# Fused attention, MLP and top-1 experts: output rows turned in 32 by 32 blocks and written in 128-byte pieces, in place of TensorE transposes

## The chip, the cores and the metric

One core of one Trainium2 chip runs the whole program in one launch. The metric is device time in microseconds (us) of that core, the median of several runs. Engines are named TensorE (PE in the rows, its weight loads PEld), VectorE (DVE), ScalarE (ACT), GpSimd (POOL) and SyncE (SP, which here only issues transfers).

## What is computed

```python
# q, k, v: (2, 12, 448, 64); x: 896 tokens x 768
scores = cap * tanh(q k^T / 8 / cap);  attn = softmax(scores);  x = attn v      # rows of 768
x = relu(x @ w_in) ** 2 @ w_out                                                # w_in 768x2048, w_out 2048x768
xn = x / (norm(x, axis=-1) + 1e-6);  en = expert_emb / (norm + 1e-6)             # 8 experts
logits = xn @ en.T / tau;  e = argmax(logits);  gate = softmax(logits)[e]
out[t] = gate[t] * (relu(x[t] @ w1[e]) @ w2[e])                                # w1 768x1024, w2 1024x768
```

All is float32. Each product is made of three reduced-precision products (high by high, high by low, low by high part), so every weight is split into a high part `wh` and a low part `wl` first.

## The kernel before

The 896 tokens are two batches of 448 (b = 0, 1). Activations lie with features on the 128 partitions and the 448 tokens along the free axis. The stages follow each other on TensorE: attention of batch 0 (paced by VectorE, to about 70 us); attention of batch 1 woven into the MLP of batch 0 (to 235 us); the MLP of batch 1 (to 366 us); the expert of batch 0 (`expert(0)`, to 434 us); the expert of batch 1 (`expert(1)`, to the end). For each batch the kernel takes the expert that most tokens chose, runs all 448 tokens through it, and later overwrites the tokens that chose another: they are gathered from `x2d` in DRAM by an indirect transfer, run through their own expert as an extra tile (products `xo`, `xy`, woven in as "x" chunks), and scattered into `out` by GpSimd (`extra_scatter`).

- **MLP.** `h` = 16 products of 6 x 3 matmuls, `y` = 6 products (d = 0..5) of 16 x 3 matmuls. After each y product ScalarE copies PSUM to `xf` (128 features x 448 tokens). Four feature products later in the next d, `rows(d, xf)` makes `x2h`, `x2l` for the experts, and also the token-major rows: four TensorE transposes `x2t`, a ScalarE copy `xr`, one transfer to `x2d` from ScalarE's queue, and four ScalarE squares that sum each token's squares (`ssp`).
- **Router** (`router(b)`, a generator that `interleave` advances between matmuls): 12 matmuls `lg`, a copy `lgs`, four small transposes `lt`, then a chain of small VectorE and ScalarE steps to the gate and the choice of the expert.
- **Expert.** `e` = 8 products of 6 x 3 matmuls, `z` = 6 products of 8 x 3. After each z product ScalarE copies it to `of`; in the next d, `rows(d, of)` makes four TensorE transposes `ot`, one VectorE multiplication by the gate into `orow`, and for two values of d one transfer to `out` from ScalarE's queue. The last two d of batch 1 go through `merged_rows`, which merges the extra tile with TensorE's help instead of the scatter.
- **Weights.** SyncE loads chunk n+7 into `wf` once VectorE has made the low part of the chunk that had this buffer (4 or 8 chunks earlier); ScalarE (or VectorE in the second MLP) casts it to `wh`, VectorE subtracts to `wl`, three chunks ahead of TensorE. Each `yield` between matmuls emits one such step (`drip`). In the MLP of batch 0 the weights come wide (`wr`) and their float32 form is stored once to DRAM (`wk`).

The order of instructions on an engine is the order in which the code emits them; each engine goes through its own list in order, so a queue that waits at one instruction holds what stands behind it. SyncE and ScalarE issue transfers to two hardware queues.

Of the kernel before, what the change touches and what calls it, by code (L numbers as in the profile page):

```python
# [8 lines left out]
F32 = mybir.dt.float32  # L9
# [11 lines left out]
def kernel(  # L21
# [59 lines left out]

    x2d = [dram.tile([NT, DM], F32, name="x2d", tag="x2d")]


# [486 lines left out]
    def mlp(b):  # L571
# [30 lines left out]
        def rows(d, xf):  # L602
            nc.vector.tensor_copy(x2h[:, d], xf)
            nc.vector.tensor_tensor(x2l[:, d], xf, f32(x2h[:, d]), op=ALU.subtract)
            tp = ps.tile([P, NC, P], F32, tag="tr", name=f"x2t{b}_{d}", bufs=2)
            for c in range(NC):
                nc.tensor.transpose(tp[:CP, c], xf[:, c * CP:(c + 1) * CP], ident)
            xr = ev.tile([CP, NC, P], F32, tag="xr", name=f"xr{b}_{d}")
            nc.scalar.copy(xr, tp[:CP])
            nc.scalar.dma_start(  # L610
                x2d[0][b * S:(b + 1) * S, d * P:(d + 1) * P].rearrange("(c p) w -> p c w", c=NC), xr)
            sq = ev.tile([CP, P], F32, tag="sq", name=f"sq{b}_{d}", bufs=1)
            for c in range(NC):
                nc.scalar.activation(sq, xr[:, c], AF.Square, accum_out=ssp[b][:, d, c:c + 1])

# [16 lines left out]
    return_rows = []  # L632
    ssp = {b: const.tile([CP, NCC, NC], F32, tag=f"ssp{b}", name=f"ssp{b}") for b in range(B)}

# [26 lines left out]
    def router_setup():  # L661
# [11 lines left out]
        nc.gpsimd.memset(ones, 1.0)  # L673
        ent["io"], ent["em8"], ent["ones"] = io, em8, ones
        for nm, sh in (("noh", [CP, NG, E]), ("meta", [CP, NG, 4]), ("cgn", [P, NG, E])):
# [4 lines left out]
        yield  # L680
        junk = ev.tile([P, S], F32, tag="sq", name="ejunk", bufs=1)
        ss2 = small([E, 2], "ess2")
# [9 lines left out]
        nc.vector.tensor_scalar(emb_s, emb_s, rn, None, op0=ALU.mult)  # L692
        yield
        tp = ps.tile([P, NCC, E], F32, tag="tr", name="ent_p", bufs=2)
# [27 lines left out]
    def router(b):  # L722
# [14 lines left out]
        nc.vector.tensor_reduce(ss, ssp[b].rearrange("p d c -> p c d"), axis=AX.X, op=ALU.add)  # L737
        yield
        lt = ps.tile([P, NC, 2, E], F32, tag="tr", name=f"lt{b}", bufs=2)
        for c in range(NC):  # L740
            nc.tensor.transpose(lt[:CP, c].rearrange("p t e -> p (t e)"), lgs[:, c * CP:(c + 1) * CP], ident[:2 * E, :2 * E])
        rn = yield from newton_sqrt(ss, [CP, NC], f"t{b}")
        sh = [CP, NC, E]
        L = small(sh, f"L{b}")
        nc.vector.tensor_copy(L, lt[:CP, :, 0])
        nc.vector.tensor_tensor(L, lt[:CP, :, 1], L, op=ALU.add)
        nc.vector.tensor_tensor(L, L, rn.unsqueeze(2).to_broadcast(sh), op=ALU.mult)
# [30 lines left out]
        rt["gate", b] = gate  # L778
        nc.vector.tensor_copy(rt["meta"][:, g, 1], gate)
        yield  # L780


# [177 lines left out]
    def expert(b, po):  # L960
# [19 lines left out]
        rest(*late.pop())  # L980
        orow = po.tile([CP, NC, DM], F32, tag="orow", name=f"orow{b}")
        pend = None
        gate = rt["gate", b]
        cut = {2: 0, 5: 3} if b < B - 1 else {2: 0, 3: 3}
        outb = out[b * S:(b + 1) * S].rearrange("(c p) w -> p c w", c=NC)

        def rows(d, of):
            tp = ps.tile([P, NC, P], F32, tag="tr", name=f"ot{b}_{d}", bufs=2)
            for c in range(NC):
                nc.tensor.transpose(tp[:CP, c], of[:, c * CP:(c + 1) * CP], ident)  # L990
            nc.vector.tensor_tensor(orow[:, :, d * P:(d + 1) * P], tp[:CP],
                                    gate.unsqueeze(2).to_broadcast([CP, NC, P]), op=ALU.mult)
            if d in cut:
                dd = slice(cut[d] * P, (d + 1) * P)
                nc.scalar.dma_start(outb[:, :, dd], orow[:, :, dd])

        def place(d):

            xm = ps.tile([P, NC, P], F32, tag="tr", name=f"xm{d}", bufs=2)
            for c in range(NC):  # L1000
                nc.tensor.matmul(xm[:CP, c], rt["smt"][:, c], rt["done"][1][:, d * P:(d + 1) * P], start=True, stop=True)
            nc.scalar.copy(orow[:, :, d * P:(d + 1) * P], xm[:CP])

        def merged_rows(d, of):

            dd = slice(d * P, (d + 1) * P)
            tp = ps.tile([P, NC, P], F32, tag="tr", name=f"ot{b}_{d}", bufs=2)
            for c in range(NC):
                nc.tensor.transpose(tp[:CP, c], of[:, c * CP:(c + 1) * CP], ident)
            xr = orow[:, :, dd]  # L1010
            for c in range(NC):
                nc.vector.scalar_tensor_tensor(xr[:, c], tp[:CP, c], rt["km"][:, c:c + 1], xr[:, c], op0=ALU.mult,
                                               op1=ALU.add)
                if c % 2:
                    e = nc.scalar if c == 1 else nc.sync
                    e.dma_start(outb[:, c - 1:c + 1, dd], xr[:, c - 1:c + 1])
# [4 lines left out]
        for d in range(NCC):  # L1021
            o = acc(f"z{b}_{d}")
            for f in range(NFE):
                if f % 4 == 0:
                    wh, wl = next_w()
                pass3(o[:, :S], wh[:, f % 4], wl[:, f % 4], gh[:, f], gl[:, f], f == 0, f == NFE - 1)
                yield "unit" if f == 3 else None
                if f == 3 and pend is not None:
                    (merged_rows if is_merged(pend[0]) else rows)(*pend)
                    pend = None  # L1030
                    yield "rows"
                if f in (1, 4) and b == B - 1 and d == NCC - 1:
                    place(d if f == 4 else d - 1)
            of = ev.tile([P, S], F32, tag="r", name=f"of{b}_{d}")
            if b == B - 1 and d == NCC - 1:
# [62 lines left out]
    def r0():  # L1098
        yield from router_setup()
        extra_setup()  # L1100
        yield from router(0)
        yield from wait(2)
        expert_value(0, rt["esi", 0])

    interleave(mlp(1), 192, r0(), 27)
    eng["hi"] = "act"
# [7 lines left out]
    def r1x():  # L1114
# [3 lines left out]
        for y in xgen["g"]:  # L1118
            yield
            if y == "gathered":  # L1120
                break
        yield from wait(2)
        expert_value(1, rt["esi", 1])
        expert_value("x", rt["tei"])
# [70 lines left out]
```

## Time and profile before

| | us |
|---|---|
| median of 3 runs (518.08 to 521.16) | 519.54 |
| time of the profiled execution | 517.91 |
| its span, first to last instruction | 516.2 |
| TensorE busy | 504.6 (98%) |
| VectorE, ScalarE, GpSimd busy | 369.6, 282.8, 62.4 |
| bytes moved | 83.62 MB, 58834 of 128909 pieces under 512 B |

About 1.7 us of the profiled execution's time lie outside the span; it is the shortest of the four times.

### The profile page before, as it was taken

The page shows a single profiled execution, that of the slowest core. Times are in us where ns is not written, and L with a number is a line of the kernel's source. Part 1 is how long each engine was busy: PE and PEld are TensorE (multiplying, and loading weights), DVE is VectorE, ACT ScalarE, POOL GpSimd, SP SyncE. Part 2 cuts the span into 40 slices and gives each one's busy share as a digit, 9 for nine tenths or more (in the row PEclk, how much of TensorE's full clock was granted, in tenths as well). Part 3 has the DMA queues.
Part 4 walks back from the last instruction along what each step waited for, and adds up shares of the span by engine and source line. Part 5 has one row for each costly group of instructions (what it writes and reads, how often), then busy time and mean ns, then how long its engine had stood idle before and what let it go on. Part 6 is the DMA issues. An engine that isn't in the chain of part 4 may idle for free.

```text
span 516.2 us, 8318 instructions
## 1 busy us (share of the span) xinstructions
PE 504.6 (98%) x2898; PEld 462.1 (90%) x2898; DVE 369.6 (72%) x715; ACT 282.8 (55%) x521; POOL 62.4 (12%) x101
## 2 busy tenths in 40 slices
PE   6999999999999999999999999999999999999995
PEld 5999989999999999999998999999899898998993
DVE  6999999898989888754786674756268344456662
ACT  4989986887866887745244232223353233444531
POOL 4655533011110010002000000000000000000000
PEclk9999999999999999999999999999999999999998
DMA  8987969799586968765233124346422345645651
GB/s 126 197 173 159 215 139 246 224 232 295 153 216 193 270 210 255 219 196 178 88 122 121 49 75 140 107 134 162 137 77 66 105 143 161 197 137 155 214 153 41
DMA packets 128909, 83.62 MB, mean 162 GB/s; under 512 B 58834, under 2 KB 116050, under 8 KB 128864
## 3 DMA queue, kind: packets, MB, share of 16 engines
q1 hardware_dynamic: 119344, 77.50, 54.2%
q10 hardware_dynamic: 9392, 5.52, 4.0%
q8 instruction: 24, 0.39, 0.3%
q14 instruction: 21, 0.17, 0.1%
q0 software_dynamic: 128, 0.04, 0.0%
HBM read 65.10 MB, written 18.28 MB: 162 GB/s over the span
## 4 chain that ended last, share of the span: by engine, by line
PE 85%; DVE 10%; DMA 1%; issue 1%; ACT 1%; DVEq 0%; ACTq 0%; POOLq 0%
PE h L564 8%; PE y L564 8%; PE h L566 8%; PE h L565 8%; PE y L566 8%; PE y L565 8%; PE pv L451 6%; PE z L564 4%; PE e L564 4%; PE e L565 4%; PE e L566 4%; PE z L566 4%; PE z L565 4%; PE sc L430 3%; DVE tq L377 2%; DVE kp L410 1%
## 5 line engine op out<-in xcount | busy, mean ns | idle before, releaser
L234 DVE TENSOR_TENSOR wl<-wf,wh 128x512 fp32r<-128x512 f32 (+1 forms) x140 | 113.9, 825 | 48.0 <-ACT wh L228 46.7
L228 ACT CAST wh<-wf 128x512 fp32r<-128x512 f32 (+1 forms) x97 | 65.8, 697 | 21.3 <-PE z L566 8.8
L564 PE MATMUL y<-gh,wh 128*128 128x448 f32 x192 | 72.4, 377 | 0.0
L564 PE MATMUL h<-xh,wh 128*128 128x448 f32 x192 | 71.7, 374 | 0.0
L566 PE MATMUL h<-xl,wh 128*128 128x448 f32 x192 | 70.2, 366 | 0.0
L565 PE MATMUL h<-xh,wl 128*128 128x448 f32 x192 | 70.2, 366 | 0.0
L566 PE MATMUL y<-gl,wh 128*128 128x448 f32 x192 | 70.2, 365 | 0.0
L565 PE MATMUL y<-gh,wl 128*128 128x448 f32 x192 | 70.1, 365 | 0.0
L451 PEld LDWEIGHTS pv<-vt,p_t 128*112 128x112 f32 x576 | 63.0, 178 | 3.0 <-PE sc L430 1.0
L451 PE MATMUL pv<-vt,p_t 128*112 128x65 f32 x576 | 62.2, 259 | 0.7 <-DMA vt<-in_v_dram 0.7
L432 ACT ACTIVATE p_t<-sc,rcap 128x448 f32<-128x448 f32 x84 | 49.0, 630 | 14.5 <-PE sc L430 14.5
L433 ACT ACTIVATE p_t<-p_t,capb 128x896 f32<-128x896 f32 x42 | 43.9, 1045 | 1.4
L396 POOL TENSOR_TENSOR ql<-tq,qh 64x448 fp32r<-64x448 f32 x23 | 27.8, 1210 | 126.8 <-ACT qh L412 67.1
L594 ACT ACTIVATE r<-h 128x448 f32<-128x448 f32 x32 | 17.2, 538 | 41.4 <-PE h L566 29.2
L230 DVE CAST wh<-wf 128x512 fp32r<-128x512 f32 (+1 forms) x43 | 21.9, 509 | 24.7 <-PE y L566 19.8
L430 PE MATMUL sc<-qh,kp 128*128 128x448 f32 x96 | 37.0, 385 | 2.5 <-DVE kp L389 1.5
L566 PEld LDWEIGHTS h<-xl,wh 128*128 128x128 f32 x192 | 36.0, 188 | 3.1
L566 PEld LDWEIGHTS y<-gl,wh 128*128 128x128 f32 x192 | 36.0, 188 | 3.0
L564 PEld LDWEIGHTS h<-xh,wh 128*128 128x128 f32 x192 | 36.1, 188 | 2.9
L565 PEld LDWEIGHTS h<-xh,wl 128*128 128x128 f32 x192 | 36.1, 188 | 2.7
L565 PEld LDWEIGHTS y<-gh,wl 128*128 128x128 f32 x192 | 36.2, 188 | 2.5
L564 PEld LDWEIGHTS y<-gh,wh 128*128 128x128 f32 x192 | 36.1, 188 | 2.5
(241 smaller groups left out, 938.0 us busy)
## 6 DMA issues: line engine op xcount, KB each, us to landing
wr<-in_moe_w_in_dram SPq DMA_DIRECT2D x16, 768.0 KB, 5.6
wr<-in_moe_w_out_dram SPq DMA_DIRECT2D x24, 512.0 KB, 4.4
wf<-in_moe_w_dram SPq DMA_DIRECT2D x24, 384.0 KB, 3.8
wf<-in_moe_w_dram SPq DMA_DIRECT2D x36, 256.0 KB, 3.1
wk<-wf SPq DMA_DIRECT2D x16, 384.0 KB, 5.7
wk<-wf SPq DMA_DIRECT2D x24, 256.0 KB, 4.8
wf<-wk SPq DMA_DIRECT2D x16, 384.0 KB, 3.5
wf<-wk SPq DMA_DIRECT2D x24, 256.0 KB, 2.9
```

Of the source, the lines that this page charges most:

```text
L228: nc.scalar.copy(c["hi"], c["f"])
L230: nc.vector.tensor_copy(c["hi"], c["f"])
L234: nc.vector.tensor_tensor(c["lo"], c["f"], f32(c["hi"]), op=ALU.subtract)
L396: nc.gpsimd.tensor_tensor(ql[D:], tq[:D], f32(qh[:D]), op=ALU.subtract)
L430: nc.tensor.matmul(sc[:, :S], h[0][:, c * P:(c + 1) * P], h[x], start=t == parts[0][0] and x == 1, stop=t == parts[-1][0] and x == 2)
L432: nc.scalar.activation(p_t[:, j], sc[:, :S], AF.Tanh, scale=rcap)
L433: nc.scalar.activation(p_t, p_t, AF.Exp, scale=capb)
L451: nc.tensor.matmul(o, w, x, start=i == 0 and t % 2 == 0, stop=i == NK - 1, skip_group_check=True)
L564: nc.tensor.matmul(o, wh, xh, start=first, stop=False)
L565: nc.tensor.matmul(o, wl, xh, start=False, stop=False)
L566: nc.tensor.matmul(o, wh, xl, start=False, stop=last)
L594: nc.scalar.activation(r, o[:, :S], AF.Relu)
```

## The change

Token-major rows are no longer made on TensorE.

- **MLP rows.** VectorE's stream transpose turns `xf` in 32 by 32 blocks: afterwards a partition holds token t of each block of 32 tokens, and 32 features of it in a run. Four transfers of 32 partitions (`store_turned`, all on SyncE's queue) write 448 runs of 128 bytes each to `x2d`. The transposes, the copy, the four accumulating squares and the transfer on ScalarE's queue go.
- **Squares.** ScalarE squares `xf` whole; GpSimd adds the six tiles up (`ssq`); one matmul with a column of ones sums over the partitions into row 32 of the router's PSUM tile, and the router's four small transposes carry that row along (33 rows in place of 16).
- **Expert rows.** VectorE turns z straight from PSUM, multiplies by the gate in the turned order (`gq`), and `store_turned` writes it to `out`. ScalarE's copy `of`, the transposes `ot` and the transfers on ScalarE's queue go, except in `merged_rows`, which keeps them. The gate reaches the turned order through DRAM (`gtd`: one store, four loads of 4-byte pieces for each batch, on SyncE's queue).
- The side generator of the second MLP is advanced 33 rather than 27 times per 192 steps; buffers are renamed.

```diff
+    def store_turned(dst, x):
+        for i in range(P // SQ):
+            nc.sync.dma_start(dst[i], x[i * SQ:(i + 1) * SQ])
...
         def rows(d, xf):
             nc.vector.tensor_copy(x2h[:, d], xf)
             nc.vector.tensor_tensor(x2l[:, d], xf, f32(x2h[:, d]), op=ALU.subtract)
-            tp = ps.tile([P, NC, P], F32, tag="tr", name=f"x2t{b}_{d}", bufs=2)
-            for c in range(NC):
-                nc.tensor.transpose(tp[:CP, c], xf[:, c * CP:(c + 1) * CP], ident)
-            xr = ev.tile([CP, NC, P], F32, tag="xr", name=f"xr{b}_{d}")
-            nc.scalar.copy(xr, tp[:CP])
-            nc.scalar.dma_start(
-                x2d[0][b * S:(b + 1) * S, d * P:(d + 1) * P].rearrange("(c p) w -> p c w", c=NC), xr)
-            sq = ev.tile([CP, P], F32, tag="sq", name=f"sq{b}_{d}", bufs=1)
-            for c in range(NC):
-                nc.scalar.activation(sq, xr[:, c], AF.Square, accum_out=ssp[b][:, d, c:c + 1])
+            xr = ev.tile([P, NS, SQ], F32, tag="xr", name=f"xr{b}_{d}")
+            nc.vector.transpose(xr.rearrange("p s d -> p (s d)"), xf)
+            store_turned(x2d[0][b * S:(b + 1) * S, d * P:(d + 1) * P].rearrange("(s t) (i d) -> i t s d", t=SQ, d=SQ), xr)
+            sq = ev.tile([P, S], F32, tag="sq" if d else "ss", name=f"sq{b}_{d}", bufs=1)
+            nc.scalar.activation(sq, xf, AF.Square)
+            if d:
+                nc.gpsimd.tensor_tensor(ssq[b], ssq[b], sq, op=ALU.add)
+            else:
+                ssq[b] = sq
...
         yield
-        lgs = ev.tile([2 * E, S], F32, tag="lgs", name=f"lgs{b}", bufs=1)
-        nc.scalar.copy(lgs, lg[:2 * E, :S])
+        NR = SQ + 1
+        nc.tensor.matmul(lg[SQ:NR, :S], ent["col"], ssq[b], start=True, stop=True)
+        lgs = ev.tile([NR, S], F32, tag="lgs", name=f"lgs{b}", bufs=1)
+        nc.gpsimd.memset(lgs[:SQ], 0.0)
+        nc.scalar.copy(lgs[:2 * E], lg[:2 * E, :S])
+        nc.scalar.copy(lgs[SQ:NR], lg[SQ:NR, :S])
+        yield
+        lt = ps.tile([P, NC, NR], F32, tag="tr", name=f"lt{b}", bufs=2)
+        for c in range(NC):
+            nc.tensor.transpose(lt[:CP, c], lgs[:, c * CP:(c + 1) * CP], ident[:NR, :NR])
...
-        def rows(d, of):
-            tp = ps.tile([P, NC, P], F32, tag="tr", name=f"ot{b}_{d}", bufs=2)
-            for c in range(NC):
-                nc.tensor.transpose(tp[:CP, c], of[:, c * CP:(c + 1) * CP], ident)
-            nc.vector.tensor_tensor(orow[:, :, d * P:(d + 1) * P], tp[:CP],
-                                    gate.unsqueeze(2).to_broadcast([CP, NC, P]), op=ALU.mult)
-            if d in cut:
-                dd = slice(cut[d] * P, (d + 1) * P)
-                nc.scalar.dma_start(outb[:, :, dd], orow[:, :, dd])
+        def rows(d, o):
+            tt = ev.tile([P, NS, SQ], F32, tag="xr", name=f"ot{b}_{d}")
+            nc.vector.transpose(tt.rearrange("p s d -> p (s d)"), o[:, :S])
+            t = po.tile([P, NS, SQ], F32, tag="ot", name=f"oq{b}_{d}", bufs=3)
+            nc.vector.tensor_tensor(t, tt, rt["gq", b].unsqueeze(2).to_broadcast([P, NS, SQ]), op=ALU.mult)
+            store_turned(outq[d * P // SQ:(d + 1) * P // SQ], t)
```

How the change moves instructions is seen at three places. First TensorE in the MLP of batch 1, where the second y product (`y_1`, inputs `gh` and `gl`) goes over to its next weight chunk. Before:

```order
L565 MATMUL y_1_3427<-gh_2749,wl_3379 128x448
L566 MATMUL y_1_3427<-gl_2750,wh_3374 128x448
L607 MATMUL x2t_0_3448<-ident,xf_0_3425 112x128 x4
L564 MATMUL y_1_3427<-gh_2749,wh_3392 128x448
L565 MATMUL y_1_3427<-gh_2749,wl_3397 128x448
```

Now:

```order
L573 MATMUL y_1_3409<-gh_2728,wl_3377 128x448
L574 MATMUL y_1_3409<-gl_2729,wh_3372 128x448
L572 MATMUL y_1_3409<-gh_2728,wh_3390 128x448
L573 MATMUL y_1_3409<-gh_2728,wl_3395 128x448
L574 MATMUL y_1_3409<-gl_2729,wh_3390 128x448
```

The four transposes between the chunks are gone and nothing stands in their place. Second, TensorE in the router of batch 1, woven into the first products e_0 and e_1 of expert 0; `sq_0` is the sum of squares, `lgs` the tile that ScalarE copies. Now:

```order
L574 MATMUL e_0_3878<-x2l_1840,wh_3823 128x448
L745 MATMUL lg_3908<-sq_0_3436,col 1x448
L572 MATMUL e_1_3933<-x2h_1839,wh_3841 128x448
L573 MATMUL e_1_3933<-x2h_1839,wl_3846 128x448
L574 MATMUL e_1_3933<-x2l_1840,wh_3841 128x448
L572 MATMUL e_1_3933<-x2h_1839,wh_3841 128x448
L573 MATMUL e_1_3933<-x2h_1839,wl_3846 128x448
L574 MATMUL e_1_3933<-x2l_1840,wh_3841 128x448
L572 MATMUL e_1_3933<-x2h_1839,wh_3841 128x448
L573 MATMUL e_1_3933<-x2h_1839,wl_3846 128x448
L574 MATMUL e_1_3933<-x2l_1840,wh_3841 128x448
L753 MATMUL lt_3950<-ident,lgs_3929 112x33 x4
```

The product of the squares is new, and nine matmuls lie between it and the transposes that need its copy; six e_0 matmuls stand ahead of it behind the 12 `lg` matmuls, and nine e_0 matmuls between the place where `rows(5)` is emitted and `lg`, as before. Third, SyncE in the z products of expert 1, where weight chunks (`wf`, numbered) are loaded. Before:

```order
L218 DMA wf128_4943<-in_moe2_w2_dram 128x4x128
L218 ISA
L218 DMA wf129_4958<-in_moe2_w2_dram 128x768
L218 ISA
L218 DMA wf130_4994<-in_moe2_w2_dram 128x768
```

Now:

```order
L226 DMA wf129_4922<-in_moe2_w2_dram 128x768
L90 DMA out_0_dram<-oq1_0_4941 32x14x32 x4
L226 ISA
L226 DMA wf130_4960<-in_moe2_w2_dram 128x768
L226 ISA
L226 DMA wf131_4976<-in_moe2_w2_dram 128x4x128
L226 ISA
L226 DMA wf132_4991<-in_moe2_w2_dram 128x768
L226 ISA
L226 DMA wf133_5004<-in_moe2_w2_dram 128x768
L90 DMA out_0_dram<-oq1_1_5012 32x14x32 x4
```

Two groups of four stores, `oq1_0` and `oq1_1`, now stand between weight loads on SyncE's queue with ten loads (130 to 139) behind the first; the other two groups of this stage come behind the last load. All 22 groups are placed like this.

## Rows read from the trace of the kernel before

**Rows 1.** The page: the span, and the chain that ended last, shares by engine.

```profile
span 516.2 us, 8318 instructions
PE 85%; DVE 10%; DMA 1%; issue 1%; ACT 1%; DVEq 0%; ACTq 0%; POOLq 0%
```

**Rows 2.** Busy time by stretch: MLP 0's y, expert 0's z, expert 1's z.

```profile
core 0: us, PE busy (x) PEld busy (x) DVE busy (x) ACT busy (x) POOL busy (x), PEclk, DMA share, GB/s
172.00:235.00 63.00, 63.00 (x399) 58.84 (x398) 49.07 (x93) 45.05 (x98) 5.32 (x15) 1.00 0.74 225
...
402.00:434.00 32.00, 31.79 (x169) 28.60 (x169) 12.79 (x21) 10.25 (x18) 1.02 (x1) 1.00 0.39 119
...
476.00:498.00 22.00, 22.00 (x123) 20.63 (x122) 15.39 (x24) 11.51 (x19) 0.00 (x0) 1.00 0.65 205
```

**Rows 3.** Timeline of TensorE, MLP of batch 1 (start us, us, instruction).

```profile
327.24 0.36 PE L566 MATMUL y<-gl,wh 128*128 128x448 f32 x1
327.44 0.60 PE L607 MATMUL x2t<-ident,xf 128*112 128x128 f32 x4
327.80 0.45 PE L564 MATMUL y<-gh,wh 128*128 128x448 f32 x1
328.08 0.37 PE L565 MATMUL y<-gh,wl 128*128 128x448 f32 x1
```

**Rows 4.** Timeline of TensorE at the two stage ends, batch 1's MLP and expert 0.

```profile
366.09 0.36 PE L566 MATMUL e<-x2l,wh 128*128 128x448 f32 x1
...
367.16 0.36 PE L565 MATMUL e<-x2h,wl 128*128 128x448 f32 x1
...
433.07 0.40 PE L888 MATMUL xo<-wl,th 128*128 128x512 f32 x1
...
434.37 0.37 PE L565 MATMUL e<-x2h,wl 128*128 128x448 f32 x1
```

**Rows 5.** Timeline of TensorE in attention: float32 products of 130 and 65 columns.

```profile
111.11 1.05 PE L451 MATMUL pv<-vs,p_t 128*112 128x130 f32 x8
111.99 0.91 PE L451 MATMUL pv<-vt,p_t 128*112 128x65 f32 x8
```

**Rows 6.** Groups by line and form: busy us, mean ns, idle before, releaser.

```profile
L607 PE MATMUL x2t<-ident,xf 128*112 128x128 f32 x48 | 7.3, 274 | 0.0
L609 ACT COPY xr<-x2t 112x512 f32<-112x512 f32 x12 | 7.0, 585 | 15.8 <-PE x2t L607 15.8
L614 ACT ACTIVATE sq<-xr 112x128 f32<-112x128 f32 x48 | 14.9, 311 | 5.8 <-ACT xr L609 4.7
L377 DVE STREAM_TRANSPOSE tq<-qk 128x448 f32<-128x448 f32 x24 | 15.2, 633 | 0.1
L991 DVE TENSOR_TENSOR orow<-ot,gate 112x512 f32<-112x512 f32 x10 | 6.9, 689 | 9.2 <-PE ot L990 9.2
L396 POOL TENSOR_TENSOR ql<-tq,qh 64x448 fp32r<-64x448 f32 x23 | 27.8, 1210 | 126.8 <-ACT qh L412 67.1
```

**Rows 7.** DMA of 1 to 6 us, when nearly all pieces have 128 bytes.

```profile
DMA packets 4928, 0.66 MB, mean 132 GB/s; under 512 B 4928, under 2 KB 4928, under 8 KB 4928
q1 hardware_dynamic: 3568, 0.44, 61.2%
```

**Rows 8.** DMA of 500.4 to 505 us: one store of 512-byte pieces.

```profile
q10 hardware_dynamic: 464, 0.23, 19.6%
```

**Rows 9.** Transfers of the tile out_dram: issue time on SyncE, min, median, max.

```profile
L1016 SPq DMA_DIRECT2D out_dram<-orow x2: 350/352/355, 506.7 to 511.6; - x2
```

**Rows 10.** Expert 1's z: SyncE's, ScalarE's, VectorE's, TensorE's timeline, weight chunks.

```profile
485.90 0.93 SPq L218 DMA_DIRECT2D wf<-in_moe_w_dram  x2
488.93 0.62 ACT L228 CAST wh<-wf 128x512 fp32r<-128x512 f32 x1
489.81 0.83 ACT L228 CAST wh<-wf 128x768 fp32r<-128x768 f32 x1 [0.26 <-DMA wf<-in_moe_w_dram]
493.67 1.14 ACT L228 CAST wh<-wf 128x512 fp32r<-128x512 f32 x2 [3.03 <-DVE orow L991]
494.32 1.29 DVE L234 TENSOR_TENSOR wl<-wf,wh 128x512 fp32r<-128x512 f32 x2 [1.12 <-ACT wh L228]
495.64 0.37 PE L565 MATMUL z<-hh,wl 128*128 128x448 f32 x1
```

**Rows 11.** Who SyncE waited for between 476 and 498 us; landing of loads there.

```profile
SPq L218 <- DVE wl L234: 11.8, 6, 3.8
wf<-in_moe_w_dram SPq DMA_DIRECT2D x5, 384.0 KB, 3.4
```

More of the change, by code (lines that the diff above doesn't have):

```diff
@@ L82 @@
     x2d = [dram.tile([NT, DM], F32, name="x2d", tag="x2d")]
+    gtd = [dram.tile([S], F32, name=f"gtd{b}", tag=f"gtd{b}") for b in range(B)]
+    NS = S // SQ
+    def store_turned(dst, x):
+        for i in range(P // SQ):
+            nc.sync.dma_start(dst[i], x[i * SQ:(i + 1) * SQ])
     order = [(b, h) for b in range(B) for h in range(H)]
@@ L632 @@
     return_rows = []
-    ssp = {b: const.tile([CP, NCC, NC], F32, tag=f"ssp{b}", name=f"ssp{b}") for b in range(B)}
+    ssq = {}
     ent = {}
@@ L673, in router_setup @@
         nc.gpsimd.memset(ones, 1.0)
-        ent["io"], ent["em8"], ent["ones"] = io, em8, ones
+        col = small([P, 1], "col")
+        nc.gpsimd.memset(col, 1.0)
+        ent["io"], ent["em8"], ent["ones"], ent["col"] = io, em8, ones, col
         for nm, sh in (("noh", [CP, NG, E]), ("meta", [CP, NG, 4]), ("cgn", [P, NG, E])):
@@ L692, in router_setup @@
         nc.vector.tensor_scalar(emb_s, emb_s, rn, None, op0=ALU.mult)
-        yield
+        yield from wait(2)
         tp = ps.tile([P, NCC, E], F32, tag="tr", name="ent_p", bufs=2)
@@ L744, in router @@
         L = small(sh, f"L{b}")
[L745 to L746 removed]
+        nc.vector.tensor_copy(L, lt[:CP, :, :E])
+        nc.vector.tensor_tensor(L, lt[:CP, :, E:2 * E], L, op=ALU.add)
         nc.vector.tensor_tensor(L, L, rn.unsqueeze(2).to_broadcast(sh), op=ALU.mult)
@@ L779, in router, with gate_turned @@
         nc.vector.tensor_copy(rt["meta"][:, g, 1], gate)
+        nc.sync.dma_start(gtd[b].rearrange("(c p) -> p c", p=CP), gate)
         yield
+    def gate_turned(b):
+        gq = small([P, NS], f"gq{b}")
+        for i in range(P // SQ):
+            nc.sync.dma_start(gq[i * SQ:(i + 1) * SQ], gtd[b].rearrange("(s t) -> t s", t=SQ))
+        rt["gq", b] = gq
     def extra_setup():
@@ L980, in expert @@
         rest(*late.pop())
-        orow = po.tile([CP, NC, DM], F32, tag="orow", name=f"orow{b}")
         pend = None
-        gate = rt["gate", b]
-        cut = {2: 0, 5: 3} if b < B - 1 else {2: 0, 3: 3}
         outb = out[b * S:(b + 1) * S].rearrange("(c p) w -> p c w", c=NC)
-        def rows(d, of):
-            tp = ps.tile([P, NC, P], F32, tag="tr", name=f"ot{b}_{d}", bufs=2)
-            for c in range(NC):
-                nc.tensor.transpose(tp[:CP, c], of[:, c * CP:(c + 1) * CP], ident)
-            nc.vector.tensor_tensor(orow[:, :, d * P:(d + 1) * P], tp[:CP],
-                                    gate.unsqueeze(2).to_broadcast([CP, NC, P]), op=ALU.mult)
-            if d in cut:
-                dd = slice(cut[d] * P, (d + 1) * P)
-                nc.scalar.dma_start(outb[:, :, dd], orow[:, :, dd])
+        outq = out[b * S:(b + 1) * S].rearrange("(s t) (k d) -> k t s d", t=SQ, d=SQ)
+        orow = {}
+        def rows(d, o):
[4 more added lines that the diff above has]
+            store_turned(outq[d * P // SQ:(d + 1) * P // SQ], t)
         def place(d):
@@ L1001, in place @@
                 nc.tensor.matmul(xm[:CP, c], rt["smt"][:, c], rt["done"][1][:, d * P:(d + 1) * P], start=True, stop=True)
-            nc.scalar.copy(orow[:, :, d * P:(d + 1) * P], xm[:CP])
+            orow[d] = po.tile([CP, NC, P], F32, tag="orow", name=f"orow{d}", bufs=2)
+            nc.scalar.copy(orow[d], xm[:CP])
         def merged_rows(d, of):
@@ L1014, in merged_rows @@
                 if c % 2:
-                    e = nc.scalar if c == 1 else nc.sync
+                    e = nc.scalar if c == 1 and d == NCC - 1 else nc.sync
                     e.dma_start(outb[:, c - 1:c + 1, dd], xr[:, c - 1:c + 1])
@@ L1033, in expert @@
                     place(d if f == 4 else d - 1)
+            if not is_merged(d):
+                pend = (d, o)
+                yield "unit"
+                continue
             of = ev.tile([P, S], F32, tag="r", name=f"of{b}_{d}")
-            if b == B - 1 and d == NCC - 1:
+            if d == NCC - 1:
                 hw = S // 2
@@ L1102, in r0 @@
         yield from wait(2)
+        gate_turned(0)
         expert_value(0, rt["esi", 0])
-    interleave(mlp(1), 192, r0(), 27)
+    interleave(mlp(1), 192, r0(), 33)
     eng["hi"] = "act"
@@ L1122, in r1x @@
         yield from wait(2)
+        gate_turned(1)
         expert_value(1, rt["esi", 1])
```

8 lines of the change are left out of this document (3 added, 5 removed).

## Prediction

> **What bounds the kernel.** I read the chain that ended last first: 85% of it is TensorE, and the 10% of VectorE lie in the first 70 us, in attention, which this change doesn't touch [rows 1]. Then the busy time by stretch, for the three stages in which rows are made: TensorE is busy for 63.00 of 63 us, 31.79 of 32 and 22.00 of 22, while VectorE has 78%, 40% and 70%, ScalarE 72%, 32% and 52%, and the DMA engines 74%, 39% and 65% [rows 2]. So a microsecond taken out of TensorE's list after 173 us is a microsecond of the kernel, as long as nothing that TensorE needs comes later. What could come later are the weights: casts, subtractions and, in expert 1's z products, the loads themselves [rows 10].
>
> **What TensorE loses.** Start to start, the matmul ahead of a group of transposes and the second one behind it are 327.24 and 328.08 apart, 0.84 us [rows 3]. Two plain matmuls take two steps of 0.20 (see 327.24 to 327.44 for one). A group therefore costs 0.44 us, more than its four instructions seem to take, since the next product starts slowly too. There are 12 groups `x2t` (48 transposes, [rows 6]) and 10 groups `ot`; 8 transposes of `merged_rows` stay. Two groups stand at the end of a stage and wait for ScalarE's copy: from 366.09 to 367.16 is 1.07 us, or 0.67 over two plain steps, and from 433.07 to 434.37 is 1.30, or 0.87 over a 512-column step of 0.23 and a plain one [rows 4]. Those waits go as well, because the products behind them don't need the copy. Sum: 20 x 0.44 + 0.67 + 0.87 = **10.3 us less**.
>
> **What TensorE gets.** Two products of 448 float32 columns for the squares. No row shows one. Eight float32 products of 130 columns take 111.11 to 111.99, 0.110 us each [rows 5]; by columns 448 take 0.38. Lower bound: 0.20, a step of the split products [rows 3]; upper bound, if a wide float32 product went four times as slowly as a split one, 0.8. I take 0.38, since this is the row of the same data type: **0.8 us more** for two, 0.4 to 1.6 as bounds. The router's transposes stay four, as short as before. They now wait for two copies of ScalarE that can only start after the product of the squares, with nine matmuls (1.8 us) as cover; at 0.5 to 0.6 us for a copy (the larger `xr` copy took 0.585, [rows 6]) plus a weight cast of 0.83 that may stand ahead [rows 10], the cover can fail in batch 1. I take **0.2 us**, bounds 0 and 0.8. The product of the squares itself stands 27 matmuls (5.4 us) behind the place where `rows` is emitted; a square of some 0.58 us and one GpSimd addition fit. That addition is not shown either: the 64 x 448 one takes 1.21 us [rows 6], and I bound it with 1.2 and 2.4.
>
> **The other engines.** ScalarE loses 12 x (0.585 + 4 x 0.311 and more, less one square) and ten copies; it was not the limit, so I count nothing, but in expert 1 one gain is real: a store on its queue waited for VectorE and held two casts for 3.03 us, so that the subtraction of 494.32 + 1.29 = 495.61 us came 0.03 us ahead of the product at 495.64 [rows 10]. VectorE gets 12 turns of 0.63 and ten times a turn plus a multiplication of about 0.69 in place of one multiplication [rows 6]: 22 x 0.63 = 14 us, 3 us of them in MLP 0's y stretch with 14 us idle, 1.9 in expert 1's with 6.6 idle [rows 2]. A turn from PSUM is not shown; between 0.63 and twice that it stays hidden on average, so nothing in the sum, 0 to 1 us as bounds. GpSimd was nearly idle in these stages.
>
> **The stores.** Each group moves 224 KB as 1792 pieces of 128 bytes where one row group had 448 of 512 bytes (or a third as many of 1536). What a 128-byte write costs no row shows. Reads of that size took 0.612 x 5 us x 16 engines / 3568 = 13.7 ns of an engine each [rows 7]; 512-byte writes took 0.196 x 4.6 x 16 / 464 = 31 ns [rows 8]. So 112 pieces for each engine take 1.5 us by the first price and 3.5 by the second, if a piece costs as much whatever its size. I take 1.5 to 2, near the row of the same size. The issue costs SyncE 4 x 0.352 = 1.4 us [rows 9], and the loads behind it on the same queue wait for all of that. In the two MLPs and expert 0 such a delay of about 3 us should be covered: chunks are loaded far ahead there and TensorE has chunks in hand.
>
> In expert 1's z stage the lead is thin. A load issued at 485.90 is cast at 488.93 and the next at 489.81, the latter 0.26 us late [rows 10], with landing in 3.4 us [rows 11]. SyncE waits there for VectorE for 11.8 of 22 us, six times [rows 11], about 2 us each; that absorbs most of the issue. What stays is the extra VectorE work of 0.6, some 0.6 of issue, and 1.5 to 2 of data on the same rings: 2.8 us later. Two groups have loads behind them (`oq1_0` and `oq1_1`). The casts stand three chunks ahead, which gives back one to two microseconds each time, and ScalarE's 3.03 us wait is gone. I take 0.6 us for each, **1.2 us**; bounds 0 and 3.3 for each (no slack, and the dear price), 6.6 in all.
>
> The gate through DRAM is needed tens of microseconds after it is written, and the loads of it stand on SyncE's queue where weights are well ahead: nothing. The tail after the last row group is the same, except that the scatter now waits for four stores issued over 1.4 us; it ends about 3 us before the last store goes out, so I count nothing there.
>
> **Sum.** 517.9 - 10.3 + 0.8 + 0.2 + 1.2 = 509.8 us, 8.1 less than the profiled execution's own time. That execution is 1.6 us below the median of the runs, 519.5, so for a median I say **511.5 us**. Bounds on the terms alone: 507.5 (0.4 for the squares, nothing late, half a microsecond back from ScalarE's freed queue) to 519.2 (1.6, 0.8, 1.0 and 6.6 more, less 10.3, with every bound at its end at once).
>
> **Rivals.**
> 1. *Loads late in the last expert.* The stores in front of the loads cost 3.3 us for each of two groups, or the same happens in expert 0's last two z products, where x chunks begin: 4 to 7 us of the 10 go back, 514 to 518 us. For it speaks the late cast [rows 10]; against it SyncE's own idle 11.8 us [rows 11].
> 2. *Slower: small writes saturate the DMA engines.* The point at which this decides can be worked out. In expert 0 a z product takes 24 x 0.20 = 4.8 us and its loads are 1024 pieces of 512 bytes, 64 for each engine, 2.0 us at 31 ns. The stores may then take 2.8 us, or 25 ns a piece. At 62 ns, twice the 512-byte write, they take 6.9, and each of eight groups (six of expert 0, two of expert 1) loses 4.1: 33 us, less about 7 that the chunks in hand cover, less the 8 above: about 530 us. For it: no write this small is in the trace. Against it: reads at 13.7 ns [rows 7]. The Trainium skill, DMA: Bandwidth & Descriptors, section Specifications, states that transfers of under 512 bytes fall short of line rate because the DMA engine then reads, modifies and writes; by that rule this rival would be the result, and no row here shows such a write.
> 3. *The full gain.* Weights never late, ScalarE's queue freed: 507 to 509.
> 4. *Nothing moves.* The gain is eaten by VectorE, which is at 78% in MLP 0's y stretch and 70% at the end [rows 2], or by rival 1 in several stages: 517 to 522. Against it: it would need 8 us of new waits on an engine that waits for almost nothing now.
>
> **Chances.** The forecast (509 to 514) 0.58; full gain 0.12; late loads (514 to 517) 0.12; no change 0.08; slower 0.10. Half a per cent, 2.6 us, is about what a measurement of this kernel can tell from no change; so faster 0.82, same 0.08, slower 0.10. The range that leaves out no more than 2 in 10 is 507.5 to 517.5: it takes in the forecast, most of the full gain and of rival 1.
>
> **What would show it.** In the profile of the changed kernel `x2t` is absent and `ot` has 8 transposes; the matmuls in the y stretch step by 0.20 without a break, so that a y product takes 48 x 0.20 = 9.7 us and not 0.44 more. The product of the squares shows 0.38 or so start to start, and no wait of TensorE ahead of it. Waits of ScalarE's casts for loads in the last expert, beyond the single 0.26 us, would show rival 1, and TensorE's wait behind them its price. A DMA share near 1 in expert 0's z stretch, and more than 25 ns for a piece, would show rival 2. I would be wrong if TensorE is idle for more than 4 us in all between 173 us and the tail, or if the first attention stage changed.

## The result, and the profile after

| | before | after |
|---|---|---|
| median of 4 runs each, us | 518.81 (517.86 to 521.16) | 513.72 (511.89 to 514.33) |
| profiled execution, its span | 517.91, 516.2 | 513.73, 512.0 |

Ratio 0.9896, 95% interval 0.9876 to 0.9916: 5.1 us faster by the medians, where 8 were forecast. The page's span and chain of the changed kernel, and its busy time in the stretches of [rows 2] (same columns):

```profile
span 512.0 us, 8172 instructions
PE 90%; DMA 4%; DVE 3%; issue 1%; ACT 0%; SPq 0%; DVEq 0%; POOLq 0%; ACTq 0%
```

```profile
172.00:235.00 63.00, 63.00 (x392) 59.05 (x391) 55.22 (x99) 40.60 (x68) 9.36 (x10) 1.00 0.79 232
402.00:434.00 32.00, 32.00 (x166) 29.19 (x165) 17.80 (x29) 7.70 (x13) 1.02 (x1) 1.00 0.69 155
476.00:498.00 22.00, 21.74 (x113) 19.42 (x112) 15.72 (x27) 8.57 (x14) 0.00 (x0) 1.00 0.70 177
```

TensorE still sets the time. VectorE has taken over 6 us of work in the first stretch, and the DMA engines are at 69% in expert 0's z in place of 39%. Transfers now hold 4% of the chain: in the first attention stage, in the last expert, and at the very end. The fall of VectorE's share of the chain from 10% to 3% is not this change's doing: it lies in the first attention stage, and four of the changed kernels below (e1, e3, e4, e6) have 9 to 11% again.

In what follows products are counted over both batches or experts: h 0 is the first h product of batch 0, z 6 to z 11 are those of expert 1. First, what went as forecast. TensorE in the MLP of batch 1, first matmul of y 8 and of y 9:

```profile
325.09 0.37 PE L572 MATMUL y<-gh,wh 128*128 128x448 f32 x1
334.82 0.36 PE L572 MATMUL y<-gh,wh 128*128 128x448 f32 x1
```

48 matmuls in 9.73 us. Before, y products of this batch started 10.2 us apart. Then the new groups (columns as [rows 6]):

```profile
L614 DVE STREAM_TRANSPOSE xr<-xf 128x448 f32<-128x448 f32 x12 | 7.7, 638 | 0.0
L1011 DVE STREAM_TRANSPOSE ot<-z 128x448 f32<-128x448 f32 x10 | 6.4, 645 | 2.4 <-PE z L574 2.4
L1013 DVE TENSOR_TENSOR oq<-ot,gq 128x448 f32<-128x448 f32 x10 | 6.2, 625 | 0.3
L619 POOL TENSOR_TENSOR sq<-sq,sq 128x448 f32<-128x448 f32 x10 | 13.9, 1386 | 160.7 <-ACT sq L617 160.7
```

A turn from PSUM (0.645 us) costs what one from SBUF does, and GpSimd's addition (1.39 us) lies near its lower bound of 1.2. The last group of stores stands alone, from 496.35 to 500 us (DMA view):

```profile
DMA packets 1856, 0.23 MB, mean 63 GB/s; under 512 B 1856, under 2 KB 1856, under 8 KB 1856
q1 hardware_dynamic: 1856, 0.23, 40.8%
```

0.408 x 3.65 us x 16 engines / 1856 = 12.8 ns for a written 128-byte piece, beside 13.7 for a read one [rows 7]. The Trainium skill's rule on transfers under 512 bytes (DMA: Bandwidth & Descriptors, Specifications) holds as far as these writes move 10 bytes in a ns of an engine and those of [rows 8] 16.5; but the piece is cheaper, not dearer.

Now what did not. TensorE around the product of the squares in batch 0:

```profile
281.19 0.37 PE L574 MATMUL h<-xl,wh 128*128 128x448 f32 x1
281.49 0.91 PE L745 MATMUL lg<-sq,col 128*1 128x448 f32 x2
282.33 0.47 PE L572 MATMUL h<-xh,wh 128*128 128x448 f32 x1
282.64 0.36 PE L573 MATMUL h<-xh,wl 128*128 128x448 f32 x1
282.84 0.36 PE L574 MATMUL h<-xl,wh 128*128 128x448 f32 x1
```

From 281.19 to 282.84 is 1.65 us; less three plain steps it is 1.04: 0.84 for the product and 0.10 on either side of it. The program issues one instruction here and the trace shows two (`x2`). Next, TensorE's first matmuls of h 16 and h 17:

```profile
241.37 0.37 PE L572 MATMUL h<-xh,wh 128*128 128x448 f32 x1
245.09 0.37 PE L572 MATMUL h<-xh,wh 128*128 128x448 f32 x1
```

The same two before the change:

```profile
242.47 0.36 PE L564 MATMUL h<-xh,wh 128*128 128x448 f32 x1
246.12 0.36 PE L564 MATMUL h<-xh,wh 128*128 128x448 f32 x1
```

18 steps in 3.72 us, 206.7 ns each; before the change they took 3.65, 202.7 ns each, with the same clock of 1.00. The slower pace holds in two stretches, from 231.7 to 264 us and from 286 to 315, 293 steps in all: 1.2 us. Then expert 1's z, ScalarE, SyncE and TensorE:

```profile
483.08 1.74 ACT L236 CAST wh<-wf 128x768 fp32r<-128x768 f32 x2 [1.59 <-DMA wf<-in_moe_w_dram]
486.06 0.62 ACT L236 CAST wh<-wf 128x512 fp32r<-128x512 f32 x1 [1.24 <-DMA wf<-in_moe_w_dram]
478.99 2.09 SPq L90 DMA_DIRECT2D out_dram<-oq  x4
481.99 6.37 SPq L226 DMA_DIRECT2D wf<-in_moe_w_dram  x6
486.73 0.47 PE L572 MATMUL z<-hh,wh 128*128 128x448 f32 x1
487.45 0.47 PE L573 MATMUL z<-hh,wl 128*128 128x448 f32 x1 [0.26 <-DVE wl L242]
```

What ScalarE's casts waited for between 476 and 498 us, before and now (us in total, times, longest):

```profile
ACT wh L228 <- DMA wf<-in_moe_w_dram: 0.3, 1, 0.3
ACT wh L236 <- DMA wf<-in_moe_w_dram: 7.5, 5, 3.7
```

Casts now wait for loads five times, 7.5 us in all, and TensorE stands still behind two of them. Last, the end: from the start of z 11 to the start of the last instruction of all, 0.05 us before the end of the span, it takes 16.01 us, and 14.97 before ("the end" in what follows). The DMA view of 506 to 510 us (first GB/s in 40 slices of 0.1 us, then a queue and an issue), and under it the same issue before the change:

```profile
GB/s 0 0 0 0 0 0 0 0 113 225 215 246 210 220 369 210 200 195 174 77 15 0 0 0 0 82 26 10 5 5 15 10 0 0 0 0 0 0 0 0
q8 instruction: 1, 0.02, 1.8%
out_dram<-orow SPq DMA_DIRECT2D x1, 112.0 KB, 3.3
```

```profile
out_dram<-orow SPq DMA_DIRECT2D x1, 112.0 KB, 2.1
```

The last store lands after 3.3 us (2.1 before), and its last few KB trickle in behind a gap. Queue q8 brings program: one piece, 1.8% of 16 engines x 4 us = 1.15 us, holds an engine from 507.45 to 508.60 us, and the last fourteen pieces of 512 bytes, a sixteenth of the store, begin at 508.60.

### The profile page after: what moved, and what is told of

The parts are those of the page before. It is cut to its first block, busy times and chain, and to the rows that moved or that the text cites. A ratio compares the mean times of both kernels' runs of the same rounds, so it can differ in the third digit from the quotient of the medians.

```text
span 512.0 us, 8172 instructions
## 1 busy us (share of the span) xinstructions
PE 499.4 (98%) x2814; PEld 454.7 (89%) x2814; DVE 386.1 (75%) x737; ACT 260.8 (51%) x417; POOL 76.0 (15%) x114
## 4 chain that ended last, share of the span: by engine, by line
PE 90%; DMA 4%; DVE 3%; issue 1%; ACT 0%; SPq 0%; DVEq 0%; POOLq 0%; ACTq 0%
PE pv L459 13%; PE h L572 8%; PE y L572 8%; PE h L574 8%; PE h L573 8%; PE y L573 8%; PE y L574 8%; PE sc L438 7%; PE e L572 4%; PE e L573 4%; PE e L574 4%; PE z L572 3%; PE z L573 3%; PE z L574 3%; DMA wf<-in_moe_w_dram 1%
## 5 line engine op out<-in xcount | busy, mean ns | idle before, releaser
L230 ACT ACTIVATE wf<-wr 128x512 f32<-128x512 f32 (+1 forms) x36 | 27.0, 750 | 22.9 <-DMA wr<-in_moe_w_out_dram 11.4
## 6 DMA issues: line engine op xcount, KB each, us to landing
wr<-in_moe_w_out_dram SPq DMA_DIRECT2D x24, 512.0 KB, 4.5
```

Source lines behind the costliest of these rows:

```text
L230: nc.scalar.mul(c["f"], c["parts"][:, :, :, 1].bitcast(F32), 2.0 ** -112)
```

## The experiments

Each ran beside the kernel before, on the same chip; ratios are to it.

| run | median us | ratio, 95% interval |
|---|---|---|
| e1, squares split | 511.99 | 0.9867, 0.9844 to 0.9890 |
| e2, one extra transpose twice | 513.21 | 0.9894, 0.9872 to 0.9916 |
| e3, stores on ScalarE's queue | 523.53 | 1.0102, 1.0075 to 1.0128 |
| e4, experts' stores twice | 524.52 | 1.0104, 1.0076 to 1.0131 |
| e5, stores by GpSimd | 512.66 | 0.9895, 0.9868 to 0.9922 |
| e6, stores later | 512.98 | 0.9895, 0.9864 to 0.9925 |
| e7, two groups of stores left out | 512.69 | 0.9893, 0.9862 to 0.9924 |
| e8, end later | 512.15 | 0.9876, 0.9861 to 0.9890 |
| e9, combined | 509.42 | 0.9832, 0.9819 to 0.9845 |
| e10, the changed kernel again | 513.77 | 0.9906, 0.9892 to 0.9920 |
| e11, MLP part alone | 518.66 | 1.0008, 0.9993 to 1.0023 |
| e12, MLP part alone, end later | 517.38 | 0.9974, 0.9957 to 0.9991 |

**The squares (e1).**

```diff
-        nc.tensor.matmul(lg[SQ:NR, :S], ent["col"], ssq[b], start=True, stop=True)
+        nc.vector.tensor_copy(qh, ssq[b])
+        nc.vector.tensor_tensor(ql, ssq[b], f32(qh), op=ALU.subtract)
+        nc.tensor.matmul(lg[:SQ + 2, :S], ent["col"], qh, start=False, stop=False)
+        nc.tensor.matmul(lg[:SQ + 2, :S], ent["col"], ql, start=False, stop=True)
```

> The squares' sum goes through TensorE as a high and a low float32r part, accumulated in the same 34 rows as the logits, in place of one float32 product; two VectorE instructions make the parts, and one ScalarE copy takes the place of two. Theory A, the float32 product itself is the step that was sized wrongly: in the changed kernel the matmul ahead of it and the second one behind it start at 281.19 and 282.84, 1.65 us apart, less three plain steps of 0.20 that is 1.04 us for one product. As two split products it is 2 x 0.20 = 0.41, so 0.63 less for each batch, 1.3 us in all: 512.4 us at a median of 513.7 now, ratio about 0.987. Theory B, the product costs 0.38 as forecast and the rest is a wait for the sum of squares: then the gap stays, since the sum comes no earlier, and the time is 513.7 or more, ratio 0.990 or above.

511.99 us. TensorE in batch 0:

```profile
280.66 0.37 PE L574 MATMUL h<-xl,wh 128*128 128x448 f32 x1
280.87 0.36 PE L753 MATMUL lg<-qh,col 128*34 128x448 f32 x1
281.07 0.36 PE L754 MATMUL lg<-ql,col 128*34 128x448 f32 x1
281.27 0.37 PE L572 MATMUL h<-xh,wh 128*128 128x448 f32 x1
```

Two plain steps, 0.41 us, and no gap on either side; nothing waited. Theory A: it was the product itself.

**The pace (e2).**

```diff
+    def one_turn(n):
+        tp = ps.tile([P, P], F32, tag="tr", name=f"turn{n}", bufs=2)
+        nc.tensor.transpose(tp, ident, ident)
...
+            if b == 1 and f == 0:
+                one_turn("a")
...
+        if b == 0:
+            one_turn("b")
```

> One extra transpose of a 128x128 constant on TensorE, with no reader, ahead of the first h product of batch 1 and another behind the router's transposes of batch 0. Theory A: a run of matmuls keeps the pace that it starts with, 206.7 ns a step or 202.7, until something else than such a matmul comes; the removed groups of transposes had let each run start anew. Then the h products of batch 1 go from 3.72 us back to 3.65 in one stretch or in both, 0.6 us less for each, and an extra transpose costs 0.1 to 0.45: between -1.0 and +0.3 us in all, 512.7 to 514.0 us. Theory B: the slower pace comes from what runs beside it (VectorE's turns, the stores, GpSimd's additions): the steps stay at 206.7 ns and the time is 0.2 to 0.9 us more.

TensorE at the first of the two, and the first matmuls of h 17 and h 18:

```profile
240.64 0.36 PE L574 MATMUL y<-gl,wh 128*128 128x448 f32 x1
240.84 0.27 PE L578 MATMUL turna<-ident 128*128 128x128 f32 x1
240.87 0.46 PE L572 MATMUL h<-xh,wh 128*128 128x448 f32 x1
244.62 0.36 PE L572 MATMUL h<-xh,wh 128*128 128x448 f32 x1
248.27 0.36 PE L572 MATMUL h<-xh,wh 128*128 128x448 f32 x1
```

3.65 us again, from that transpose on and no earlier (the 46 steps ahead of it still take 206.5 ns), though all that runs beside it is the same; likewise behind the second one. So theory A holds in this: a run keeps the pace it began with. But the time hardly moved, for a reason that belongs to the theory: the next pause, the router's count at 318 us, put the 232 steps behind it into the slower pace (y products of 9.92 us and not 9.73), which takes 0.9 us. In e9 a third transpose stands there, and the steps behind it are at 202.7 again: five transposes at three places in two kernels, and five times the faster pace. What sets it at other pauses was not found, and that the removed transposes had kept the pace up is not shown: groups of four are followed by either pace (the router's `lt` by 202.7 ns before the change and by 206.6 now, two groups `ot` in e11 by 206.4 and 206.7).

**The stores' queue (e3, e5, e6) and their price (e4, e7).** In e3 `store_turned` issues on `nc.scalar`.

> All turned stores are issued on ScalarE's queue, as the row stores were before the change. Theory A, loads come late in the last expert because four stores with 0.48 us of issue each, and a wait for VectorE, stand ahead of them on SyncE's queue: casts that wait for loads go from 7.5 us (five times, 3.7 at most) to under 1 between 476 and 498 us, TensorE gets up to 1.0 us back there; ScalarE's casts are then held behind the stores (3.03 us for a group before the change, hidden but for 0.03). Time -1.0 to 0 us: 512.7 to 513.7. Theory B, the loads are late because 1792 pieces of 128 bytes share the rings with them: the casts stay late by as much, and the issue on ScalarE (12 groups in the MLPs, too) costs 0 to 3 us: 513.7 to 517.

Both theories missed: 9.8 us slower than the changed kernel. ScalarE in expert 1's z:

```profile
484.69 2.04 ACTq L90 DMA_DIRECT2D out_dram<-oq  x4
486.85 2.82 ACT L236 CAST wh<-wf 128x768 fp32r<-128x768 f32 x4 [4.76 <-issue]
495.55 2.69 ACTq L90 DMA_DIRECT2D out_dram<-oq  x4
498.36 1.14 ACT L236 CAST wh<-wf 128x512 fp32r<-128x512 f32 x2 [5.05 <-DMA out_dram<-oq]
```

The casts stand behind stores that wait for VectorE and then take 2.0 to 2.7 us to issue; ScalarE idles for 4.8 and 5.1 us, and TensorE loses 4.5 us between z 8 and z 9 and 1.5 between z 9 and z 10 against the changed kernel. By z 8 it is 2.6 us behind already, lost at the change of experts, where two more such groups stand (z 9 starts 7.1 us, z 10 8.6 us after the changed kernel's). A store of [rows 10] on this queue held two casts for 3.03 us and was covered; four issues and a longer chain on VectorE are not.

In e4 each group of the experts is written once more, to a spare tensor.

> Each group of four turned stores of the experts is written a second time, to a spare tensor; nothing else differs. Theory A, a 128-byte write costs what a 128-byte read does: 1856 pieces took 40.8% of 3.65 us on 16 engines, 12.8 ns a piece. Ten more groups are 112 pieces an engine each, 1.4 us of data and 1.9 us of issue on SyncE; an expert 0 z product of 4.8 us then has 2.0 us of loads and 2.9 us of stores, 4.9 in all, which is just about full: 0 to 0.5 us lost for each of six, 1 to 2 us for each of the two groups in expert 1 that have loads behind them: 516 to 520 us. Theory B, rival 2 of the prediction at 25 ns a piece or more: 2.8 us of data for a group, 0.8 us or more over the 4.8 for each of six, on top of what the chunks in hand cover, and the DMA share above 0.95 between 402 and 434 us: over 520 us.

524.52 us, over theory A's range and in theory B's, but not for B's reason: the DMA share between 402 and 434 us is 0.73. SyncE in expert 0's z:

```profile
424.35 0.99 SPq L227 DMA_DIRECT2D wf<-in_moe_w_dram  x2
425.43 2.23 SPq L91 DMA_DIRECT2D out_dram<-oq  x4
427.70 2.11 SPq L91 DMA_DIRECT2D spare<-oq  x4
430.06 0.98 SPq L227 DMA_DIRECT2D wf<-in_moe_w_dram  x2
```

A round of the list takes 5.7 us and a z product 4.8: SyncE's issue is full before the rings are. The chunks in hand cover it in expert 0, and the debt is paid at the start of expert 1, where casts wait for loads between 424 and 447 us:

```profile
ACT wh L237 <- DMA wf<-in_moe_w_dram: 18.3, 4, 5.3
```

The DMA share between 434 and 448 us is 0.86, so that the data may have a part in it there.

In e5 the experts' stores are issued by `nc.gpsimd`; in e6 they go out behind the last of the eight pieces of the next z product (f = 7) in place of the fourth (f = 3); in e7 two groups go nowhere.

> The experts' turned stores are issued by GpSimd, which has nothing else to do there; those of the MLPs stay on SyncE's queue. Theory A, the loads of the last expert are late because of SyncE's list (four issues of 0.48 us a group and the wait for VectorE ahead of them, 5.1 us of waiting for two groups between 476 and 498 us): the casts' 7.5 us of waiting for loads go to under 1, TensorE gets 0.5 to 1.0 us back between z 8 and z 11: 512.7 to 513.3 us. Theory B, the pieces on the rings make them late, or GpSimd's own issue of such a transfer is dear (its scatter of 64 rows stands at 0.96 us): the casts stay late, or the stores land so late that the scatter, which has to wait for them, ends the kernel: 513.7 to 520.

> The four stores of an expert's row group are emitted four steps of the z product later, so that one or two weight loads go ahead of them on SyncE's queue; the last group of either expert stays where it is. Theory A, as for the run with GpSimd: SyncE no longer waits for VectorE's multiplication with loads behind it (5.1 us in two waits now), the late casts fall from 7.5 us to under 4, and 0.3 to 1.0 us come back: 512.7 to 513.4. Theory B, it is the issue and the data of the stores wherever they stand: a store only makes the next load late instead, 513.4 to 514.5.

> The stores of the two row groups of the last expert that have loads behind them (oq1_0 and oq1_1) are left out, and with them 256 columns of batch 0's or batch 1's output. This is the price of the term that the prediction put at 1.2 us. Theory A, late loads cost about that: between z 8 and z 11 TensorE gets 0.6 to 1.2 us back, casts wait for loads under 1 us: 512.5 to 513.1 us. Theory B, the late casts are hidden by the chunks in hand and the missing time is elsewhere (the squares' product and the pace): 513.4 to 514.

By the medians the three can't be told from the changed kernel (0.9893 to 0.9895). The traces show more. First matmul of z 8 and of z 11, in the changed kernel and in e7:

```profile
475.05 0.37 PE L572 MATMUL z<-hh,wh 128*128 128x448 f32 x1
495.96 0.36 PE L572 MATMUL z<-hh,wh 128*128 128x448 f32 x1
```

```profile
474.36 0.37 PE L572 MATMUL z<-hh,wh 128*128 128x448 f32 x1
494.37 0.36 PE L572 MATMUL z<-hh,wh 128*128 128x448 f32 x1
```

By the traces the three agree to 0.01 us: from z 8 to z 11 they take 20.00, 20.01 and 20.01 us, the changed kernel 20.91, again (e10) 20.45, and e8, which does not touch this, 21.53. So late loads cost 0.5 to 1.5 us, differing from execution to execution, and all three edits remove it. e5 leaves the pieces on the rings and takes only their issue, with the wait ahead of it, off SyncE's list, and gains as much as e7, which has no pieces there: it is the list that makes the loads late, not the data. Whether the issue or the wait for VectorE counts more in it, these runs don't separate. My numbers for the casts missed: they still wait 5.7 us (e5), 6.5 us (e6) and 3.1 us (e7) in all, but 2.5 at most and not 3.7, and a wait that short is covered.

**The end (e8).**

```diff
+    last = ps.tile([P, 512], F32, tag="pv", name="last", bufs=2)
+    for _ in range(24):
+        nc.tensor.matmul(last[:8, :8], ident[:, :8], ident[:, :8], start=True, stop=True)
```

> Behind its last transposes TensorE gets 24 products of 8 by 8 by 8 that nothing reads; TensorE has nothing else to do there. What is tested is the end of the kernel: from the start of the last z product's 11th piece (z 11) to the end it takes 14.97 us before the change and 15.9 to 16.3 in each kernel with it, and the last store lands 3.3 us after its issue in place of 2.1. Theory A: TensorE's next 16 KB of program are fetched by one DMA engine (a piece of 16384 bytes, 1.15 us) just while that engine has its share of the last store; the fetch follows TensorE's branch at the end, so a branch that comes 1 us later moves the fetch behind the store: the last store lands in 2.1 us, the end takes 15.0 to 15.3 us, and the time is 0.7 to 1.0 us less than without. Theory B, the last store is slow for another reason, or the fetch has another trigger: the end stays at 16 us, or becomes longer by up to 1 us.

(z 11 there is the last z product.) TensorE's last row, and the last store in the DMA view of 504.8 to 508.8 us:

```profile
505.25 1.35 PE L1180 MATMUL last<-ident 128*8 128x8 f32 x48
```

```profile
out_dram<-orow SPq DMA_DIRECT2D x1, 112.0 KB, 2.0
```

The store lands after 2.0 us, no program piece of queue q8 is in the stretch (it comes at 508.85 us), and from z 11 to the end it takes 14.79 us, a little under theory A's 15.0 to 15.3. In the ten traces of changed kernels without this edit a piece starts 2.2 to 2.3 us behind TensorE's last row; here it starts 2.25 us behind the row above, so it has moved with TensorE: theory A. Instructions that compute nothing, on an engine that has nothing to do, give 1.2 us back. The Trainium skill, Runtime: NRT & Kernel Launch, Instruction fetch mechanics, tells of 16 KB blocks and of a fetch when a branch leaves the blocks in hand; the 16384 bytes and the fetch's coming later with the branch agree. The section speaks of what a fetch costs the engine that needs the program; here a store of another engine pays for it.

**Together (e9).** e1's split, e6's later stores, three transposes, e8's end.

> Together: the squares' sum as two split products; the experts' stores four steps later; an extra transpose ahead of the first h product of batch 1, behind the router's transposes and behind the count of batch 0; the 24 small products at the end. By the runs so far: 1.3 to 1.7 us for the squares, 0.9 for the late loads, about 1.2 for the pace less 0.36 for three transposes, and 0.7 to 1.0 for the end if theory A of the run before holds: 3.6 to 4.4 us below the changed kernel, 508.8 to 509.6 us at a median of 518.3 for the kernel before, ratio 0.981 to 0.984. If the parts don't add (another stretch falls into the slower pace, a load comes late elsewhere), 510 to 511.5.

509.42 us, ratio 0.9832: the parts add. From z 8 to z 11 20.07 us, the end 14.82, TensorE busy for 22.00 of 22 us between 476 and 498. It is the fastest of all, 4.35 us below the changed kernel as run beside it (e10).

> The changed kernel once more, unchanged, for a second trace beside these runs. If the 0.5 us by which its first trace was behind at 71 us, and again at 98 us, are that execution's own, they are not there now (h 0 at 71.0 to 71.1 us); all else stays: pace 206.7 ns in the same two stretches, 1.04 us for each product of the squares, 0.9 us late in the last expert, 16.0 us for the end. 512.7 to 513.7 us.

513.77 us; the pace, the squares and the end (16.16 us) are the same again. The start is not: h 0 begins at 72.6 us here, at 72.9 in e12 and between 70.9 and 71.3 in the ten other runs, so the 0.5 us of the first trace (71.6; ahead of it TensorE waits 1.9 us for a load of attention, `vt`, and 0.7 before the change) are that execution's own. Of the next 0.5 us that is not shown: from h 4 to h 5 (93 to 98 us) it takes 4.64 us before the change, 4.95 to 5.54 in twelve of the thirteen traces of changed kernels and 4.43 in e12, and one trace of the kernel before can't tell whether the change costs this.

**One part alone (e11, e12).** The MLPs and the router as changed, the experts as before; e12 adds e8's edit.

> The change of the MLPs and the router alone; the experts make their rows by TensorE's transposes as before the change. By the prediction's terms: 11 x 0.44 + 0.67 less, 0.8 for the squares and 0.2 for the router more, 4.5 us less than before, ratio 0.991. By what the traces show now: two products of the squares at 1.04 and 1.2 us of slower pace (an upper value, since a later pause can end it) go against the 5.5, so 2.2 us less, ratio 0.996; the end may differ by 1 us either way. Between 0.9935 and 0.991 the first holds, above 0.994 the second.

1.0008, above 0.994, but no gain at all where the second sum had 2.2 us. z 11 starts 1.37 us before that of the kernel before, 0.8 less than my 2.2, and then the end takes 16.92 us in place of 14.97, with the last store 3.7 us under way behind a fetch of 1.55 us (the 4.4 named below is an earlier store's).

> The MLPs' and the router's part of the change alone, as in the run before, with the 24 small products behind TensorE's last transposes. In that run TensorE reached z 11 at 499.76 us, 1.37 before the kernel before (501.13), yet from there to the end it took 16.92 us in place of 14.97, the last store 4.4 us to land. Theory A: this part's gain was real and was eaten at the end by the fetch of TensorE's program; with the fetch behind the last store the end takes 14.7 to 15.1 us and the kernel is 1.2 to 2.0 us faster than before, ratio 0.996 to 0.998. Theory B: the part is worth nothing by itself: ratio 0.9995 or more.

0.9974; the end takes 15.22 us, just over theory A's 15.1, and the last store lands after 2.0 us: theory A. The gain is that of the medians, whose intervals just part (0.9993 to 1.0023 and 0.9957 to 0.9991); the trace kept of e12 is of its slowest execution (519.53 us). A gain of 1.3 us, near the 1.37 by which e11 reached z 11 early, had been lost to the fetch at the end.

## Why the prediction was right, and by how much it was not

**What bounds the kernel, and what TensorE loses: right.** From 173 to 496 us TensorE is idle for 0.26 us in all, where 4 would have spoken against it. Product starts move by 0.37 to 0.59 us for a group where 0.44 was taken, and by 1.21 at expert 0's end (0.44 + 0.87 forecast). VectorE's turns, GpSimd's additions and the gate through DRAM are hidden, as said. No wait for the two copies ahead of `lt` shows, where 0.2 was taken.

**What TensorE gets: the step that failed.** 0.8 us for two products, 2.1 measured, above the upper bound of 1.6. I divided the rows of attention by their count: "eight float32 products of 130 columns take ... 0.110 us each" [rows 5]. They are four. A float32 product is two entries in the trace: each of the two products of the squares shows as two, e8's 24 as 48, and the program has 48 of 130 columns where the trace has 96. So 130 columns cost 0.22, 448 by columns 0.76 (0.84 measured), and the changes from split products and back 0.10 each.

**Loads behind stores: right in size and place.** 1.2 forecast for two groups, 0.5 to 1.5 measured (0.9 in the first trace), in the last expert. The greatest term of the 2.8 us behind that forecast, 1.5 to 2 us of data on the rings, was not what made them late (e5). That data would be the limit (rival 2) is refuted at 12.8 ns a piece against the 25 from which it would decide. The resource next to full is SyncE's list: I took 0.352 us for an issue, these take 0.478 (median).

**"The tail ... is the same": wrong by 1.0 us.** TensorE's instructions are the same and at the same distances (8.97 and 8.98 us from z 11 to the last transpose). One store of `merged_rows` has moved from ScalarE's queue to SyncE's, which the section on the change does not name; that is not the cause, since e11 has it back on ScalarE's queue and has the late end. The program fetch was not looked at. Nor was the pace: I took the step of [rows 3] for a constant, and it is one of two.

Of the profiled execution's 513.7 us against 509.8 forecast: squares +1.3, pace +1.2, end +1.0, start +0.9 (0.5 at h 0, this execution's own, and 0.4 from there to 156 us, set beside the one trace of before), late loads -0.3, copies -0.2: 3.9. The three terms that were in no sum (pace, end, start) make 3.1 of it.

That the median, 513.7, lies inside the forecast's 509 to 514 is in part luck. The 1.6 us that were added to 509.8, for the step from the profiled execution to the median, were not there in the changed kernel, whose profiled execution lies at its median. The prediction's bounds mix these two footings as well: 507.5 is counted from 517.9 and 519.2 from 519.5; from 517.9 both would be 507.5 and 517.6.

## What to carry to other kernels

Before dividing a duration by a count of rows, hold the count against the program's. When TensorE is the bound, taking instructions off its list changes more than their time: the pace of the run behind them and the place of its program fetches, each worth a microsecond here, so compare the starts of equal products and the landing of the last store, not only busy time. Ahead of loads on one queue it is the issue of many small transfers, and the wait ahead of them, that counts first, and the engine whose queue they stand on.

## What the runs showed of the hardware

- Matmuls of 128x448 in a row step by 202.7 or by 206.7 ns at a granted clock of 1.00, for as long as nothing else comes between (runs of up to 250 steps); one float32 transpose, 0.12 us, was followed by the faster pace five times out of five, a group of four by either.
- A float32 product of 448 columns costs 1.04 us of TensorE between split ones, five plain steps. The Trainium skill, FP8 and Floating Point Precision, TensorE Precision Notes, gives four passes for a float32 product; an estimate from that and the plain step, 4 x 0.203 = 0.81 us, is near the 0.84 of the product without the changes.
- A fetch of 16 KB of program, 2.2 us behind TensorE's last row, takes a DMA engine for 1.15 us (0.90 to 1.55 in the ten traces), and a store that is under way lands 1.2 us later.
